# A router's one-hot tiles held behind a weight split, and three row buffers for every later expert, in a fused attention and mixture-of-experts kernel

## The chip, the cores and the metric

One core of a Trainium2 chip runs the whole program in one launch. The metric is the device time of an execution in microseconds; the time of a kernel is the median of several executions on the chip.

## The reference

Three layers follow each other on 8 x 576 = 4608 tokens of 512 channels. The change lies in the second one.

```python
def _attn_ref(q, k, v, phi):          # per batch and head
    a = phi - np.max(phi, axis=2, keepdims=True)
    ...
    k_m = np.einsum('bhsm,bhsd->bhmd', a, k)
    v_m = np.einsum('bhsm,bhsd->bhmd', a, v)
    ...
    return np.matmul(attn, v_m)

def _moe_ref(x, w_gate, w1, w2):      # 8 experts, 576 tokens each
    logits = x @ w_gate
    order = np.argsort(-logits.flatten())
    ...
    for idx in order:                 # best pair first, until an expert is full
        tok, e = (int(idx) // E, int(idx) % E)
        if assigned[tok] >= 0 or counts[e] >= cap:
            continue
        assigned[tok] = e
        counts[e] += 1
    ...
    for e in range(E):
        mask = assigned == e
        h = np.maximum(x[mask] @ w1[e], 0.0)
        out[mask] = h @ w2[e]

def _moe2_ref(x, w_in, w_out):        # dense, 512 to 2048 and back
    h = x @ w_in
    g = h * np.clip(h + 3.0, 0.0, 6.0) / 6.0
    return g @ w_out
```

## The kernel before, in words

The first part (the attention, lines up to 530) writes the rows x to a DRAM tensor xd and keeps the logits LG on the chip. The second part is built by a small planner. The main line issues the matmuls of the experts in order; beside it run generators (routes, gathers, weights, dense_max, dense, and the evictions), which issue their instructions when the planner's clock CK.now says that their inputs are there. So the order in each engine's queue is decided when the program is built, by estimated times; on the chip each engine works through its own queue in that order and waits by semaphores.

Every product is made of float16 pieces: a matrix is scaled by a power of two and split into a high and a low half (the high half by ScalarE, ACT, the low half by VectorE, DVE, as a scalar_tensor_tensor; a few by GpSimd, POOL), and three matmuls take the place of one.

- `route(k)` (L737) finds the expert that fills next and its 576 tokens: eight steps of a search (C, counts on TensorE into rtp, flags FL, mi), then the counts ce, the totals tot, and six one-hot tiles OH of 128 x 768, made by VectorE in `oh` (L926), each followed by six small matmuls OH x RH (L952). From their sum come the row indices ix{k}.
- `gathers` (L1056) fetches the 576 rows of expert k from xd in five indirect transfers issued on POOL (xg), transposes them on TensorE (xp), and splits them into xt. Experts 2 to 7 have two buffers (depth 2): the third transfer waits for the first transpose. Expert 1 has all five at once, three of them in staging buffers of the weights (wst0, wst1), which it borrows.
- `weights` (L984) fetches the weights T = 2k (first layer) and T = 2k+1 (second layer) of expert k in four chunks wst0 to wst3 (POOL transfers), sums their squares, reduces these to one scale s over all partitions (pow2, all_max L688: a matmul amx against the identity), and splits the chunks into w_0 to w_3. The set W2[k] is marked when all four are split. T = 3 waits until expert 1 has its rows under way (XI), since it needs the borrowed buffers.
- `mm_slot` (L631) hands out the four PSUM slots that the layers' tiles, the transposes and the reductions share. MMQ lists who holds one. When four are taken, the next caller takes the oldest entry out of the list and waits for it; while it waits, the generators go on, and one of them can find three entries and take a slot.
- `l1(k)` and `l2(k)` are the two layers of expert k: 16 tiles of 12 matmuls and 8 tiles of 24, so 192 matmuls of 128 x 288 each. Expert 0 takes the first layer four tiles at a time. After two experts, `l34` runs the dense layers on their 1152 tokens; its matmuls need the dense weights, which `dense_piece` (L1206) brings in 32 pieces through VectorE (a shift and three or four cva steps each), in the gaps, with spare buffers named by `spare` (L1147).

Nearly all instructions behind line 550 carry the line of a helper: L567 for VectorE, ScalarE and GpSimd, L618 for the layers' matmuls, L623 for transposes, L694 for the reductions amx.

Of the kernel before, what the change touches and what calls it, by code (L numbers as in the profile page):

```python
# [9 lines left out]
F32 = mybir.dt.float32  # L10
F16 = mybir.dt.float16
BF16 = mybir.dt.bfloat16
# [8 lines left out]
def attn_moe_kernel(ctx: ExitStack, tc: tile.TileContext, q, k, v, phi, w_gate, w1, w2, w_in, w_out, out):  # L21
    nc = tc.nc
# [3 lines left out]
    NT = 36  # L26
# [603 lines left out]

    def mm_slot(done):  # L631
        while len(MMQ) >= 4:
            d = MMQ.pop(0)
            b, CK.busy = CK.busy, False
            need(lambda: d[0])
            CK.busy = b
        MMQ.append(done)

    def mm_tile(shape, name, done):
# [22 lines left out]
    nc.vector.tensor_scalar(triu, jp, 0.0, None, op0=OP.is_lt)  # L662
    onesb = rt.tile([128, 128], BF16, name="onesb")
    nc.vector.memset(onesb, 1.0)
    ones72 = rt.tile([128, 2 * NT], F32, name="ones72")
    nc.vector.memset(ones72, 1.0)
    wE = rt.tile([128, E], F32, name="wE")
    nc.vector.tensor_scalar(wE, iT[:, 0:E], -1.0, float(E), op0=OP.mult, op1=OP.add)
    pb = rt.tile([128, 4], F32, name="pb")
# [67 lines left out]
    def route(k):  # L737
# [121 lines left out]
        else:  # L859
# [11 lines left out]
        V_.scalar_tensor_tensor(G[:, 0], V, thf, be, op0=OP.is_gt, op1=OP.mult)  # L871
        V_.scalar_tensor_tensor(G[:, 1], V, thf, be, op0=OP.is_equal, op1=OP.mult)
        sc = rt.tile([128, 2, NT], F32, name="scn")
        V_.tensor_tensor_scan(sc.rearrange("p a t -> p (a t)"), ones72, G.rearrange("p a t -> p (a t)"), 0.0,
                              op0=OP.mult, op1=OP.add)
        tot = rt.tile([128, 2], BF16, name="tot")
        V_.tensor_copy(tot, sc[:, :, NT - 1])
# [46 lines left out]
        p = ps.tile([128, 64], F32, name="rtp")  # L924

        def oh(q4):  # L926
            o = rt.tile([128, 6, 128], BF16, name="OH", bufs=3)
            V_.tensor_tensor(o, lo[:, 6 * q4:6 * q4 + 6, None].to_broadcast([128, 6, 128]),
                             i128[:, None, :].to_broadcast([128, 6, 128]), op=OP.is_equal)
            return o  # L930
        yield V_.t - 0.3
        OH = [oh(0)]
        if k == 0:
            lof = hbuf(2)[:, 0:6]
# [49 lines left out]
    def weights():  # L984
        for T in range(2 * E):
            k, which = divmod(T, 2)
            while k not in EIX or T == 3 and 1 not in XI:
                yield CK.now + 0.3
            for c in range(4):
                if T == 0 and c == 2:  # L990
# [24 lines left out]
            for n in range(9):  # L1015
                if n < 8:
                    c, i = divmod(n, 2)
                    if i == 0:
                        tl.append(wk.tile([128, 2, 1024], F16, name=f"w{which}_{c}"))
                    cs = slice(i * 512, i * 512 + 512)  # L1020
                    if n in PS.get(T, ()):
                        A_.activation(WST[T, c][0][:, cs], WST[T, c][0][:, cs], AF.Copy, scale=s[:, 0:1])
                        yield A_.t - 0.3
                        A_.activation(tl[c][:, 0, cs], WST[T, c][0][:, cs], AF.Copy)
                    else:
                        A_.activation(tl[c][:, 0, cs], WST[T, c][0][:, cs], AF.Copy, scale=s[:, 0:1])
                    rd.append(A_.t + HOP)
                if n and n - 1 in PS.get(T, ()):
                    yield rd[n - 1], G_
                    c, i = divmod(n - 1, 2)  # L1030
                    cs = slice(i * 512, i * 512 + 512)
                    G_.tensor_tensor(tl[c][:, 1, cs], WST[T, c][0][:, cs], tl[c][:, 0, cs], op=OP.subtract)
                    yield CK.now + 0.1, A_
                    WC[T] = c + i, tl
                elif n:
                    yield rd[n - 1], V_
                    c, i = divmod(n - 1, 2)
                    cs = slice(i * 512, i * 512 + 512)
                    V_.scalar_tensor_tensor(tl[c][:, 1, cs], WST[T, c][0][:, cs], s[:, 0:1], tl[c][:, 0, cs],
                                            op0=OP.mult, op1=OP.subtract)  # L1040
                    if i and T + 1 < 2 * E and T != 2:
                        w_issue(T + 1, c)
                    yield CK.now + 0.1, A_
                    WC[T] = c + i, tl
            yield V_.t
            (W1, W2)[which][k] = tl

    XT, XI = {}, set()

    def ybuf(m):  # L1050
        return wk.tile([128, CAP], F32, name=f"y_{m}")
# [4 lines left out]
    def gathers():  # L1056
        for k in range(E):
# [7 lines left out]
            def fetch(i):  # L1065
                n = 64 if i == 4 and k % 2 == 0 else 128
                if k == 0:
                    xg = hbuf(3 + i)[:, 0:512]
                elif k == 1 and i > 1:
                    if i % 2 == 0:  # L1070
                        big.append(wk.tile([128, 2, 512], F32, name="xg", tag=f"wst{i // 2 - 1}"))
                    xg = big[-1][:, i % 2]
                else:
                    xg = wk.tile([128, 512], F32, name="xg", tag=f"xg{i % 2}")
                G_.indirect_dma_start(out=xg[:n], out_offset=None, in_=xd, in_offset=U(ap=ix[:n, i:i + 1], axis=0))
                rdy.append(dma(0.75, G_.t) + (2.2 if k > 1 else 0.0))
                xgs.append((i, n, xg))
            depth = 2 if k > 1 else 5
            big = []
            if k == 0:  # L1080
                G_.t = max(G_.t, XDT[0])
            for i in range(depth):
# [1 line left out]
                    while not SR[0]:  # L1084
                        yield CK.now + 0.1
                fetch(i)
            XI.add(k)
            while k and L1D.get(k - 1, 0) < 8:
                yield CK.now + 0.3
            xt = wk.tile([128, 2, 4, CAP], F16, name="xt")  # L1090
# [56 lines left out]
    def spare(kind):  # L1147
        tags = ["dst0", "dst1", "dst2"] if kind else ["cva0", "cva1"]
        if 1 in XT or 1 in L1D:
            tags += [] if kind else ["xg0", "xg1"]  # L1150
        if 1 in W2:
            tags += [f"wst{c}" for c in range(4)] if kind else ["wscr"]
        for t in tags:
            if t not in BUSY:
                return t
# [379 lines left out]
```

## Time and profile before

| | us |
|---|---|
| median of 3 runs | 1510.31 (1505.42 to 1511.45) |
| profiled execution | 1503.65 |
| its span | 1501.6 |
| TensorE busy in it | 1397.4 (93%) |
| VectorE busy | 835.3 (56%) |
| ScalarE busy | 732.6 (49%) |
| GpSimd busy | 487.8 (32%) |

The span is what the profiler saw on the core, 2.05 us less than the execution's own time. A busy share is the time in which an engine works on an instruction; waiting in its queue isn't counted. The attention fills about the first 225 us, expert 0 the time to 324 us, expert 1 to 380 us, the dense layers of these two follow, and from some 450 us on the pattern repeats with experts 2 and 3, 4 and 5, 6 and 7.

### The profile page before, as it was taken

The numbers are of one execution on the slowest core, as the hardware profiler recorded it, in microseconds if no ns is written. First come the engines' busy times: TensorE is split into PE (matmuls) and PEld (weight loads), VectorE is DVE, ScalarE is ACT, GpSimd is POOL, SyncE is SP. The second block draws the span as 40 slices with busy tenths as digits, with TensorE's granted clock in tenths as the row PEclk, the third lists the DMA queues.
The fourth block names the chain that finished last, engine by engine and source line by source line (L and its number), as shares of the span: only waits on it lengthen the run. The fifth ranks groups of instructions, "written<-read, shape, count | busy, mean of one in ns | idle before, by whom it ended". The sixth has DMA issues, their size and how long they took to land.

```text
span 1501.6 us, 26275 instructions
## 1 busy us (share of the span) xinstructions
PE 1397.4 (93%) x10506; PEld 931.4 (62%) x10506; DVE 835.3 (56%) x1985; ACT 732.6 (49%) x1419; POOL 487.8 (32%) x555
## 2 busy tenths in 40 slices
PE   4778886898889999999999999999999999999997
PEld 3667764777444555997555558875555588755553
DVE  4788967889995775553146755522459335221111
ACT  3667655577763563452335634523346445233332
POOL 3565305134553443301233532102325421023232
PEclk9989996999999999999999999999999999999999
DMA  9866587355310221200001311100013211000000
GB/s 299 293 231 201 158 273 248 118 185 167 114 43 22 82 84 57 86 28 2 1 22 57 109 57 51 64 1 1 22 57 110 71 39 62 1 0 22 1 21 21
DMA packets 65913, 130.67 MB, mean 87 GB/s; under 512 B 5248, under 2 KB 35968, under 8 KB 65792
## 3 DMA queue, kind: packets, MB, share of 16 engines
q1 hardware_dynamic: 49808, 74.48, 15.0%
q0 software_dynamic: 15168, 52.96, 10.9%
q8 instruction: 82, 1.34, 0.4%
q10 hardware_dynamic: 816, 1.57, 0.3%
q14 instruction: 39, 0.32, 0.1%
HBM read 110.12 MB, written 18.87 MB: 86 GB/s over the span
## 4 chain that ended last, share of the span: by engine, by line
PE 67%; DVE 14%; ACT 5%; issue 5%; DMA 4%; POOL 2%; SPq 0%; ACTq 0%; POOLq 0%; DVEq 0%
PE p L618 39%; PE acc L618 21%; DVE cva L567 4%; DMA xg<-xd,ix 2%; PE xa L420 1%; DMA ph<-in_phi_dram 1%; PE kvp L191 1%; DMA wst<-in_moe_w_dram,ei 1%; DVE w L567 1%; ACT h L567 1%; PE rtp L795 1%; DVE pm L138 1%; PE xp L623 1%; DVE h L567 1%; POOL h L567 1%
## 5 line engine op out<-in xcount | busy, mean ns | idle before, releaser
L618 PE MATMUL acc<-wo,h 128*128 128x512 f16 x1728 | 418.1, 379 | 5.2 <-ACT h L567 4.3
L618 PE MATMUL p<-yt,wi 128*128 128x384 f16 x2304 | 417.6, 327 | 0.0
L567 POOL TENSOR_TENSOR h<-h,h 128x384 f16<-128x384 f32 x192 | 187.3, 976 | 634.5 <-ACT h L567 492.6
L618 PEld LDWEIGHTS <-w 128*128 128x128 f16 x3072 | 339.1, 121 | 49.1 <-issue 4.4
L618 PEld LDWEIGHTS <-wi 128*128 128x128 f16 x2304 | 219.2, 98 | 156.0 <-issue 1.2
L567 ACT ACTIVATE h<-p,half_c,inv 128x384 f32<-128x384 f32 (+1 forms) x256 | 143.9, 587 | 278.5 <-PE p L618 271.2
L618 PEld LDWEIGHTS <-h 128*128 128x128 f16 x1728 | 163.5, 98 | 174.1 <-ACT h L567 6.0
L567 DVE SCALAR_TENSOR_TENSOR h<-h,p 128x384 f32<-128x384 f32 x192 | 105.9, 551 | 290.0 <-ACT h L567 282.7
L618 PE MATMUL p<-xt,w 128*128 128x288 f16 x1536 | 198.8, 289 | 3.7 <-DVE h L567 3.5
L618 PE MATMUL p<-h,w 128*128 128x288 f16 x1536 | 196.3, 287 | 4.3 <-DVE w L567 3.7
L567 ACT ACTIVATE h<-h 128x384 f16<-128x384 f32 x192 | 100.1, 521 | 135.7 <-DVE h L567 131.9
L567 DVE SCALAR_TENSOR_TENSOR h<-p,h 128x288 f16<-128x288 f32 x128 | 57.4, 455 | 73.6 <-ACT h L567 73.5
L567 DVE SCALAR_TENSOR_TENSOR w<-wst,s,w 128x512 f16<-128x512 f32 x124 | 96.1, 806 | 2.2 <-ACT w L567 2.2
L567 POOL DMA_INDIRECT wst<-in_moe_w_dram,ei x64 | 68.7, 1073 | 87.0 <-DVE scn L567 33.5
L567 ACT ACTIVATE h<-p 128x288 f16<-128x288 f32 x128 | 51.7, 410 | 90.8 <-PE p L618 90.8
L567 ACT ACTIVATE w<-wst,s 128x512 f16<-128x512 f32 x124 | 82.5, 712 | 7.1 <-DVE s L567 6.2
L567 DVE SCALAR_TENSOR_TENSOR cva<-dst,cva 128x512 int32<-128x512 int32 (+1 forms) x96 | 82.7, 881 | 0.5 <-ACT dst L567 0.3
L567 DVE TENSOR_REDUCE ym<-y 128x1 f32<-128x288 f32 x64 | 28.8, 450 | 91.5 <-ACT y L567 91.3
L567 ACT ACTIVATE wscr<-wst 128x1024 bf16<-128x1024 f32 x64 | 67.3, 1052 | 13.3 <-DMA wst<-in_moe_w_dram,ei 12.6
L567 ACT ACTIVATE y<-p 128x288 f32<-128x288 f32 x64 | 26.1, 407 | 96.6 <-PE p L618 95.1
L567 POOL DMA_INDIRECT xg<-xd,ix x35 | 37.2, 1064 | 75.9 <-PE xp L623 49.7
L191 PE MATMUL kvp<-kvt,A 128*64 128x128 f32 x576 | 46.0, 315 | 7.3 <-ACT A L170 3.3
(313 smaller groups left out, 1558.4 us busy)
## 6 DMA issues: line engine op xcount, KB each, us to landing
dst<-in_moe_w_out_dram SPq DMA_DIRECT2D x26, 512.0 KB, 4.3
qt<-in_q_dram SPq DMA_DIRECT2D x8, 1024.0 KB, 11.5
dq<-in_moe_w_in_dram SPq DMA_DIRECT2D x16, 512.0 KB, 5.7
xd<-xs SPq DMA_DIRECT2D x32, 256.0 KB, 5.5
kvt<-in_k_dram SPq DMA_DIRECT2D x7, 1152.0 KB, 9.1
kvt<-in_v_dram SPq DMA_DIRECT2D x7, 1152.0 KB, 11.8
dst<-in_moe_w_in_dram SPq DMA_DIRECT2D x15, 512.0 KB, 4.0
ph<-in_phi_dram SPq DMA_DIRECT2D x8, 576.0 KB, 9.8
```

Source lines behind the costliest of these rows:

```text
L138: nc.vector.tensor_reduce(pm, PH[b].rearrange("p h (r m) -> p h m r", m=M), axis=AX.X, op=OP.max)
L191: nc.tensor.matmul(p[i * 64:(i + 1) * 64, g, 0:128], A[:, hp, r, :], KV[b][:, :, hp, r * 64:(r + 1) * 64], start=(r == 0), stop=(r == R - 1))
L420: nc.tensor.matmul(p[r, g], AT[u][:, half, g, r], VB[b][:, g], start=True, stop=True)
L567: r = f(*a, **kw)
L618: nc.tensor.matmul(o, l, r, start=start, stop=stop)
L623: nc.tensor.transpose(o, i, idn)
L795: nc.tensor.matmul(p[:60, :32], C[:, 4 * t:4 * t + 4].rearrange("p t n -> p (t n)"), Bo[:, 4 * t:4 * t + 4].rearrange("p t e -> p (t e)"), ...
```

## The change

Four edits go together. In `mm_slot` a waiting caller leaves the oldest entry in the list until it is done. In `route`, the second round (k = 1) makes its one-hot tiles only after W2[0], the split second weights of expert 0, is marked, and OH has two buffers instead of three. In `gathers` every expert from 1 on has three buffers xg0 to xg2; nothing is borrowed, so `weights` drops the wait for XI and asks for T = 3 as each chunk of T = 2 is split. The third row buffer also becomes a spare buffer for cva. A tile of 72 ones gives way to columns of ones_c.

```diff
     def mm_slot(done):
         while len(MMQ) >= 4:
-            d = MMQ.pop(0)
+            d = MMQ[0]
             b, CK.busy = CK.busy, False
             need(lambda: d[0])
             CK.busy = b
+            if MMQ and MMQ[0] is d:
+                MMQ.pop(0)
         MMQ.append(done)
...
-    ones72 = rt.tile([128, 2 * NT], F32, name="ones72")
-    nc.vector.memset(ones72, 1.0)
...
         def oh(q4):
-            o = rt.tile([128, 6, 128], BF16, name="OH", bufs=3)
+            o = rt.tile([128, 6, 128], BF16, name="OH", bufs=2)
...
         yield V_.t - 0.3
+        while k == 1 and 0 not in W2:
+            yield CK.now + 0.1
         OH = [oh(0)]
...
-            while k not in EIX or T == 3 and 1 not in XI:
+            while k not in EIX:
                 yield CK.now + 0.3
...
-                    if i and T + 1 < 2 * E and T != 2:
+                    if i and T + 1 < 2 * E:
                         w_issue(T + 1, c)
...
-                elif k == 1 and i > 1:
-                    if i % 2 == 0:
-                        big.append(wk.tile([128, 2, 512], F32, name="xg", tag=f"wst{i // 2 - 1}"))
-                    xg = big[-1][:, i % 2]
                 else:
-                    xg = wk.tile([128, 512], F32, name="xg", tag=f"xg{i % 2}")
+                    xg = wk.tile([128, 512], F32, name="xg", tag=f"xg{i % 3}")
...
-            depth = 2 if k > 1 else 5
-            big = []
+            depth = 3 if k else 5
...
-            tags += [] if kind else ["xg0", "xg1"]
+            tags += [] if kind else ["xg0", "xg1", "xg2"]
```

The orders that the planner makes of it differ from the first layer of expert 0 on. On TensorE, before, the reduction for the scale of expert 0's second weights (amx from s_0m) stands between two groups of four layer tiles:

```order
L618 MATMUL p_3822<-xt,w_3_3652 128x288
L618 LDWEIGHTS w_3_3652
L618 MATMUL p_3822<-xt,w_3_3652 128x288
L694 MATMUL amx<-ident,s_0m 128x128
L813 LDWEIGHTS onesb
L813 MATMUL rtp<-FL,onesb 128x8
L618 LDWEIGHTS w_0_3574
L618 MATMUL p_3945<-xt,w_0_3574 128x288
```

Now it stands 46 layer matmuls further on, inside the next group, between the last tile's matmuls:

```order
L618 MATMUL p_3948<-xt,w_3_3650 128x288
L618 LDWEIGHTS w_3_3650
L618 MATMUL p_3959<-xt,w_3_3650 128x288
L694 MATMUL amx<-ident,s_0m 128x128
L618 LDWEIGHTS w_3_3650
L618 MATMUL p_3959<-xt,w_3_3650 128x288
L618 LDWEIGHTS w_3_3650
L618 MATMUL p_3959<-xt,w_3_3650 128x288
L795 LDWEIGHTS C
```

What moved is amx, from behind 96 to behind 142 of the 192 matmuls of that layer.

On VectorE, before, the end of the second routing round (RH, then the one-hot tiles OH) runs on with only steps of the dense pieces (cva) and maxima of y between the tiles; the halves w_0 to w_3 of expert 0's second weights stand some thirty rows ahead of this:

```order
L567 TENSOR_SCALAR lo<-sli 128x36
L567 TENSOR_SCALAR hi<-sli 128x36
L567 TENSOR_TENSOR R_4274<-hi,iTf 128x180
L567 TENSOR_TENSOR RH<-R_4274,idt 128x360
L567 TENSOR_TENSOR OH<-lo,i_2717 128x768
L567 SCALAR_TENSOR_TENSOR cva<-dst,cva 128x512
L567 TENSOR_REDUCE ym<-y_4171 128x1
L567 TENSOR_TENSOR OH<-lo,i_2717 128x768
L567 SCALAR_TENSOR_TENSOR cva<-dst,cva 128x512
L567 TENSOR_TENSOR OH<-lo,i_2717 128x768
```

Now the last two pairs of these halves, w_2 and w_3, stand between RH and the first one-hot tile:

```order
L567 TENSOR_SCALAR lo<-sli 128x36
L567 TENSOR_SCALAR hi<-sli 128x36
L567 TENSOR_TENSOR R_4213<-hi,iTf 128x180
L567 TENSOR_TENSOR RH<-R_4213,idt 128x360
L567 SCALAR_TENSOR_TENSOR w_2_4151<-wst_3673,s_0_3901,w_2_4151 128x512 x2
L567 SCALAR_TENSOR_TENSOR w_3_4219<-wst_3697,s_0_3901,w_3_4219 128x512 x2
L567 SCALAR_TENSOR_TENSOR cva<-dst,cva 128x512
L567 TENSOR_TENSOR OH<-lo,i_2717 128x768
L567 TENSOR_SCALAR cva<-dst 128x512
L567 TENSOR_TENSOR OH<-lo,i_2717 128x768
```

The one-hot tiles, and with them the six groups of matmuls on TensorE, follow the split; on TensorE the first group stands behind 15 matmuls of the second layer of expert 0, where it stood behind 63.

On POOL, before, the five gathers of expert 1's rows stand together, and the four transfers of its second weights behind them:

```order
L567 DMA wst_4236<-in_moe_w_dram,ei_4187 128x1024
L567 TENSOR_TENSOR wi_4267<-cva,wi_4267 128x512
L567 TENSOR_TENSOR wi_4402<-cva,wi_4402 128x512
L567 DMA xg<-xd,ix_4466 128x512 x5
L567 DMA wst_4592<-in_moe_w_dram,ei_4187 128x1024
L567 DMA wst_4603<-in_moe_w_dram,ei_4187 128x1024
```

Now three gathers stand together, then a subtraction of a dense piece (wi), then the other two and the first two weight transfers:

```order
L567 DMA wst_4243<-in_moe_w_dram,ei_4170 128x1024
L567 TENSOR_TENSOR wi_4266<-cva,wi_4266 128x512
L567 DMA xg<-xd,ix_4411 128x512 x3
L567 TENSOR_TENSOR wi_4404<-cva,wi_4404 128x512
L567 DMA xg<-xd,ix_4411 128x512 x2
L567 DMA wst_4509<-in_moe_w_dram,ei_4170 128x1024
L567 DMA wst_4542<-in_moe_w_dram,ei_4170 128x1024
L567 TENSOR_TENSOR wo_4526<-cva,wo_4526 128x512
```

The fourth and fifth gather moved behind that subtraction, and subtractions of dense pieces now stand among the weight transfers.

## Rows read from the trace of the kernel before

**Rows 1.** Windows: stretch, length; busy PE, PEld, DVE, ACT, POOL; PE clock, DMA, GB/s.

```profile
274.00:299.20 25.20, 21.55 (x182) 18.23 (x183) 21.71 (x67) 11.10 (x22) 4.95 (x5) 1.00 0.25 77
299.20:312.70 13.50, 13.08 (x132) 9.96 (x130) 13.05 (x31) 9.53 (x19) 3.04 (x2) 1.00 0.58 205
312.70:324.60 11.90, 9.35 (x76) 7.40 (x74) 9.58 (x20) 7.10 (x14) 6.77 (x7) 1.00 0.47 125
324.60:357.60 33.00, 27.71 (x219) 25.83 (x217) 31.80 (x64) 27.95 (x59) 12.18 (x10) 1.00 0.49 160
357.60:389.60 32.00, 26.93 (x196) 19.86 (x196) 31.86 (x52) 22.33 (x40) 15.61 (x11) 0.95 0.61 195
389.60:446.40 56.80, 51.89 (x268) 26.29 (x269) 55.97 (x79) 40.35 (x71) 32.61 (x26) 0.97 0.22 65
450.00:1501.60 1051.60, 1037.79 (x6977) 654.81 (x6975) 463.72 (x1147) 445.61 (x858) 293.14 (x313) 1.00 0.13 41
```

**Rows 2.** Waits of TensorE, 225 to 450 us: total us, times, longest.

```profile
PE amx L694 <- DVE sy_1m L567: 5.5, 1, 5.5
PE acc L618 <- ACT h L567: 4.3, 4, 1.8
...
PE p L618 <- DVE w L567: 3.7, 2, 2.3
```

**Rows 3.** Waits of TensorE, 450 us to the end.

```profile
PE xp L623 <- DMA xg<-xd,ix: 2.1, 4, 1.0
PE rtp L855 <- DVE ce L567: 1.7, 1, 1.7
```

**Rows 4.** Timeline of TensorE, 225 to 330 us: start, us, instruction, wait.

```profile
274.48 0.49 PE L694 MATMUL amx<-ident,s_0m 128*128 128x128 f32 x2 [1.11 <-DVE h L567]
...
277.62 2.00 PE L618 MATMUL p<-xt,w 128*128 128x288 f16 x15 [1.00 <-DVE h L567]
...
285.11 1.14 PE L618 MATMUL p<-xt,w 128*128 128x288 f16 x8 [1.43 <-DVE h L567]
...
292.88 0.28 PE L618 MATMUL p<-h,w 128*128 128x288 f16 x1 [0.61 <-ACT h L567]
...
296.26 4.57 PE L618 MATMUL p<-h,w 128*128 128x288 f16 x36
...
310.22 0.31 PE L952 MATMUL rtp<-RH,OH 128*128 128x10 bf16 x6 [0.24 <-DVE dmm L567]
...
316.23 0.63 PE L623 MATMUL xp<-ident,xg 128*128 128x128 f32 x4 [0.92 <-DMA xg<-xd,ix]
...
324.37 2.12 PE L618 MATMUL p<-xt,w 128*128 128x288 f16 x16
```

**Rows 5.** Timeline of VectorE, 232 to 330 us.

```profile
277.49 1.41 DVE L567 SCALAR_TENSOR_TENSOR w<-wst,s,w 128x512 f16<-128x512 f32 x2
...
299.24 0.95 DVE L567 TENSOR_TENSOR OH<-lo,i 128x768 bf16<-128x768 int32 x1
```

**Rows 6.** Timeline of GpSimd (POOL): first gather of expert 1.

```profile
312.84 0.97 POOL L567 DMA_INDIRECT xg<-xd,ix  x1 [3.49 <-DVE ix L567]
```

**Rows 7.** Windows of the cva steps on VectorE alone: busy us (steps), clock, DMA.

```profile
357.60:389.60 32.00, 28.70 (x37) 0.95 0.61 195
389.60:446.40 56.80, 45.39 (x53) 0.97 0.22 65
```

**Rows 8.** Timeline of TensorE, 326 to 452 us.

```profile
441.11 2.12 PE L618 MATMUL acc<-wo,h 128*128 128x512 f16 x9 [1.84 <-ACT h L567]
...
445.39 1.47 PE L618 MATMUL acc<-wo,h 128*128 128x512 f16 x6 [0.22 <-ACT h L567]
447.19 0.82 PE L618 MATMUL acc<-wo,h 128*128 128x512 f16 x3 [0.33 <-POOL h L567]
```

**Rows 9.** Windows around the wait at sy_1, columns as in Rows 1.

```profile
384.60:390.00 5.40, 0.04 (x1) 0.00 (x0) 5.26 (x16) 4.50 (x9) 2.38 (x2) 0.96 0.42 145
390.00:391.50 1.50, 1.41 (x5) 0.98 (x6) 1.50 (x4) 0.52 (x1) 0.46 (x1) 0.50 0.05 11
```

More of the change, by code (lines that the diff above doesn't have):

```diff
@@ L873, in route @@
         sc = rt.tile([128, 2, NT], F32, name="scn")
-        V_.tensor_tensor_scan(sc.rearrange("p a t -> p (a t)"), ones72, G.rearrange("p a t -> p (a t)"), 0.0,
+        V_.tensor_tensor_scan(sc.rearrange("p a t -> p (a t)"), ones_c[:, 0:2 * NT], G.rearrange("p a t -> p (a t)"), 0.0,
                               op0=OP.mult, op1=OP.add)
@@ L1046, in weights @@
             (W1, W2)[which][k] = tl
-    XT, XI = {}, set()
+    XT = {}
     def ybuf(m):
@@ L1086, in gathers @@
                 fetch(i)
-            XI.add(k)
             while k and L1D.get(k - 1, 0) < 8:
```

## The prediction

> **What bounds the kernel now.** I read the stretches first. From 450 us to the end TensorE (PE) is busy 1037.79 of 1051.60 us, at full clock. From 274 to 446.4 us it is VectorE (DVE) that hardly rests: it idles 3.49, 0.45, 2.32, 1.20, 0.14 and 0.83 us in the six stretches [rows 1]. So a change in the early stretch is paid in VectorE's queue, and one in the late stretch only where TensorE still waits. The waits agree: between 225 and 450 us TensorE lost 5.5 us ahead of the reduction for sy_1 (the scale of the second expert's output), 3.7 us for weight halves and 4.3 us for h tiles of the dense layers [rows 2]; after 450 us the row buffers cost it 2.1 us in four waits, the counts ce 1.7 us [rows 3]. What the edited lines can win is part of some 20 us of idle time before 450 us and of some 4 us after it.
>
> On TensorE the two programs are alike until 274 us. From there I replay the new order with the durations of the trace; positions are counted in the orders of the engines.
>
> **1. The slot rule: the second scale of expert 0 comes later.** Before, the reduction matmul for s_0 of the second weights (amx) stood behind 96 of the 192 first-layer matmuls and started at 274.48, after a wait of 1.11 us for a slot; the layer then waited 1.00 and 1.43 us for its own slots [rows 4]. Now a waiting tile of the layer keeps its place in the list, the reduction can't get in front of it, and amx stands behind 142 matmuls. The layer goes on at 273.9 instead of 275.0; its fourth tile waits for a slot until 276.3 (1.15 us, 9 matmuls done). 37 matmuls of 0.127 us (36 in 4.57 us [rows 4]), the small routing matmuls between them (0.8 us) and a wait of 0.85 us for amx's own slot put it at about 282.7, 8.2 us later. The dense reduction (dmm), which now stands two layer matmuls behind it, takes a second slot, and the next tile waits 1.1 us. In all the slots cost 3.4 us, as much as the 3.5 us before.
>
> **2. The split of those weights meets the router on VectorE.** Eight halves (two in 1.41 us [rows 5]) stood between 277.5 and 289. Now one pair stands behind the last routing step, one behind ce and two behind RH, and the gate puts the first one-hot tile (OH) behind them all. VectorE's load up to there is nearly the same (0.75 us more in small reductions, some 0.5 us less idle). The first OH, 0.95 us from 299.24 before [rows 5], ends at about 300.6: 0.4 us later.
>
> **3. TensorE stands still ahead of it.** The first layer of expert 0 ends at 291.9, the router's totals cost 0.95 us, and the second layer begins at 293.1 (before 292.88 [rows 4]). It runs 14 matmuls and waits for w_2, which follows RH: until 297.3, 2.35 us. One matmul later stands the first OH group, behind 15 second-layer matmuls where it stood behind 63: it waits until 300.7, 3.3 us. The other five groups come at TensorE's own pace (62 matmuls, 0.31 us a group [rows 4]). The last stands at 310.1, as before (310.22), but with 77 second-layer matmuls done instead of 125: 48 x 0.127 = 6.1 us behind.
>
> **4. Rows of expert 1.** The first gather can go out at 311.4 instead of 312.84 [rows 6], since fewer other steps stand between the last OH group and the indices. From that issue to the transpose at 316.23 it took 3.4 us [rows 4, 6]. With three buffers the first three go out at 311.4, 312.7 and 314.0; the last two need a buffer back, stand behind a POOL subtraction, and go out at 316.4 and 317.7. The transposes at 315.4, 316.6, 318.0, 319.9 and 321.2 cost about 2 us of waits, as many as before. The second expert's first layer, 324.37 before [rows 4], starts at 330.1: **5.7 us late**.
>
> **5. What VectorE makes of that.** Ahead of sy_1 now stand eight more steps of the dense pieces (cva), which fall into the gap that TensorE leaves. At 0.78 us a step (37 in 28.70 us), less the overlap of neighbours, 0.66; in the late stretch 0.86 (53 in 45.39 us [rows 7]): 5.3 to 6.9 us. Against them VectorE had 7.6 us of idle time up to 389.6, the first five figures of [rows 1]; in the replay 6.5 us of it remain (3 before the first OH, 2 at the transposes, 1.5 in the first layer of expert 1). So sy_1 is 5.3 - 1.1 = **4.2 us late**, at worst 5.8. TensorE's 5.7 us are not added: it waited 3.7 us for halves and 5.5 us at sy_1 [rows 2], and a late start fills these waits. If nothing of VectorE's idle time remained, sy_1 would be 2.3 us early: the lower bound.
>
> **6. The tail.** The eight steps are gone from the end, where h tiles queue behind them: TensorE's waits of 1.84, 0.22 and 0.33 us from 441 us on [rows 8] fall. The other h waits, 4.3 - 1.84 - 0.22 = 2.2 us, stand in an unchanged order and stay. **2.4 us back.**
>
> **7. Experts 2 to 7.** Three gathers stand in front where two stood; the fourth and fifth follow together. That can take at most the 2.1 us of row waits [rows 3]; the fourth still waits for a buffer. I take **1.3 us back**, between 0 and 3.8 (with ce, which moves too).
>
> At nothing: the removed memset of 72 columns (ahead of the router, nobody waits); two OH buffers (the third tile needs the first group's matmuls, over 2 us before it); the earlier request for expert 1's second weights (needed after 350); a third spare buffer for cva (pieces wait for VectorE, not for room). If the room were what held them, that is the faster rival.
>
> **Sum:** 4.2 - 2.4 - 1.3 = +0.5 us. The profiled execution took 1503.65 us, so 1504.2 on its scale; it lies 6.7 us under the median of the runs, 1510.31, and the runs spread over 6.0 us. The prediction is for a median: **1510.8 us**. I take 0.5%, 7.5 us, as what a measurement of this kernel can tell from no change.
>
> **A row against the change.** TensorE did 0.04 us of work from 384.6 to 390, and from 390 to 391.5 the granted clock was 0.50, the level of 1.2 GHz [rows 9]; by 393 this had cost 1.5 us. The new wait ahead of OH, 2.35 and 3.3 us with one matmul between, is alike. My sum leaves it out, since the matmuls behind it are tied to OH tiles; at half clock 11 of them take 2.8 us against some 1.9 us a tile, so up to 1.5 us could show. The Trainium skill (TensorE: Matmul & The Clock Gate, Part 1: The HAM clock gate) says that the throttled state is the default and that activity lifts it, so a long wait is paid twice. By that rule the sum is 0.5 + 1.5 = +2.0 us; the row at 390 agrees with it.
>
> **Rivals.**
> - *Slower: the late start is not filled.* It decides at VectorE's first h step of expert 1's first layer, near 332 us. If VectorE has run dry there, everything behind it, the second weights of expert 1 and sy_1, moves by the whole 5.7 us, and the clock is lost twice, behind OH and behind a longer wait at sy_1 (1.5 us each); the tail's gain is eaten by the pieces that then run late. +8.7 us, 1519. For it: the h steps stand in order and nothing overtakes them. Against: the replay finds VectorE busy with pieces until 331.6. Chance 0.22.
> - *Faster: VectorE's idle time goes.* A third spare buffer lets a third piece be in flight; if that fills all but 3 of the 7.6 us, sy_1 is 5.3 - 4.6 = 0.7 us late, all 4.3 us of h waits go, 3.8 us after 450, and the 1.5 us of low clock behind sy_1: -8.9 us, 1501.4. Against: much of the idle time is a wait for routing matmuls, and these stay. Chance 0.24.
> - *The gate does nothing*, the weights being split before the router gets there. VectorE's order speaks against it: w_2 and w_3 stand between RH and OH. Steps 3 and 5 would vanish: -1.3 us, within 0.5%. Chance 0.04.
>
> **The numbers.** The forecast has 0.50. The rivals lie just beyond 0.5%: of the faster one 0.20 falls outside, of the slower one 0.17, and of the forecast, by the spread of the runs, 0.05 on either side. So faster 0.25, slower 0.22, the rest 0.53. The range takes in the centres of both rivals and a little more, 1500 to 1520; beyond it I leave about 0.2.
>
> **What would show it.** Right: amx for s_0 at 281 to 284; TensorE waiting over 5 us between 294 and 301, for w and then OH; the first layer of expert 1 at 329 to 332; a wait at sy_1 that ends 2 to 6 us later; no h wait behind 441; under 1.5 us of row waits after 450. Wrong in size: a clock near 0.5 at 300 to 305, or VectorE idle by over 2 us near 332. Wrong in kind: OH groups spread over the second layer as before, or TensorE's position at 450 more than 6 us off.

## The result and the profile after

| | us |
|---|---|
| median of 7 runs, changed kernel | 1516.68 (1515.76 to 1521.18) |
| median of 7 runs, kernel before, same chip | 1506.16 (1501.62 to 1511.45) |
| ratio | 1.0068, 95% interval 1.0046 to 1.0089 |
| profiled execution and its span | 1515.76 and 1513.9 |

The changed kernel is slower by 0.68%, some 10 us. Against the runs of before beside it that is +10.5 us where +0.5 was forecast (1510.8 us, on a median of three runs that lay 4 us over the seven here). The time lies inside the range that was given, 1500 to 1520, only because that range took in the centre of the slower rival, at +8.7; the forecast's own sum missed by 10 us, so the hit of the range is luck as far as its mechanism goes.

The profiled executions don't start the experts at the same time: the first product of l1(0), up to which TensorE's order has not changed, stands at 253.78 us before and at 256.03 now. Such differences come with every profile here (the eleven below have it between 251.50 and 256.51; whether the change has a part in it isn't shown). So I count from that product, and call its time t; "on the old scale" means 2.25 us taken off. From t to the end of the span it is 1501.6 - 253.78 = 1247.8 us before and 1513.9 - 256.03 = 1257.9 now, 10.1 us more: the whole loss.

The windows of the changed kernel (columns as in [rows 1]) for the stretches behind the split of expert 0's second weights:

```profile
274.00:292.00 18.00, 15.77 (x135) 13.38 (x134) 16.21 (x50) 8.97 (x18) 1.52 (x1) 1.00 0.30 90
292.00:300.00 8.00, 3.81 (x29) 2.74 (x27) 7.62 (x27) 2.73 (x6) 0.00 (x0) 0.98 0.00 0
300.00:309.00 9.00, 6.78 (x54) 4.87 (x55) 8.22 (x13) 2.32 (x4) 7.96 (x4) 0.64 0.47 127
309.00:316.00 7.00, 3.66 (x40) 2.74 (x37) 0.00 (x0) 1.27 (x3) 1.94 (x2) 1.00 0.78 290
316.00:323.00 7.00, 5.08 (x27) 3.30 (x28) 5.55 (x16) 5.75 (x12) 1.80 (x2) 0.55 0.00 0
...
450.00:1513.90 1063.90, 1051.64 (x7054) 661.88 (x7052) 470.31 (x1157) 452.23 (x871) 295.23 (x320) 1.00 0.12 41
```

The new row is the fourth: in 309 to 316 VectorE, which idled 0.45 us in the whole of its second stretch of [rows 1], does nothing at all for 7 us. TensorE works at 0.64 and 0.55 of its clock on either side of it. The late stretch is as full as before.

The timeline of TensorE before, three rows that [rows 4] doesn't have: the first product of l1(0), the start of l2(1), and the reduction for sy_1.

```profile
253.78 0.46 PE L618 MATMUL p<-xt,w 128*128 128x288 f16 x1
...
350.86 2.25 PE L618 MATMUL p<-h,w 128*128 128x288 f16 x17
...
390.09 0.77 PE L694 MATMUL amx<-ident,sy_1m 128*128 128x128 f32 x2 [5.45 <-DVE sy_1m L567]
```

The timeline of TensorE now, with these rows and those that answer to [rows 4]:

```profile
256.03 0.46 PE L618 MATMUL p<-xt,w 128*128 128x288 f16 x1
...
285.20 0.49 PE L694 MATMUL amx<-ident,s_0m 128*128 128x128 f32 x2 [0.87 <-DVE h L567]
...
294.55 1.88 PE L618 MATMUL p<-h,w 128*128 128x288 f16 x14 [0.18 <-DVE h L567]
...
298.76 0.30 PE L618 MATMUL p<-h,w 128*128 128x288 f16 x1 [2.33 <-DVE w L567]
...
302.22 0.32 PE L954 MATMUL rtp<-RH,OH 128*128 128x10 bf16 x6 [3.16 <-DVE OH L567]
...
310.63 0.30 PE L954 MATMUL rtp<-RH,OH 128*128 128x10 bf16 x6
...
317.92 0.32 PE L954 MATMUL rtp<-RH,OH 128*128 128x10 bf16 x6 [5.26 <-DVE OH L567]
...
340.57 4.08 PE L618 MATMUL p<-xt,w 128*128 128x288 f16 x32
...
366.90 2.24 PE L618 MATMUL p<-h,w 128*128 128x288 f16 x17
...
406.27 0.76 PE L694 MATMUL amx<-ident,sy_1m 128*128 128x128 f32 x2 [5.04 <-DVE sy_1m L567]
```

The waits of 2.33 and 3.16 us for w_2 and for the first one-hot tile are there as forecast. The fifth group comes at 310.63, and then the sixth is 5.26 us late. From there on everything is late, and by the same amount: l1(1) starts at t + 84.5 where it started at t + 70.6, l2(1) at t + 110.9 where it started at t + 97.1, and the reduction for sy_1 stands at t + 150.2 where it stood at t + 136.3.

What held the sixth tile can be followed over three queues. GpSimd (POOL) first, the four loads of expert 1's first weights in the kernel before, with the first and the last load of its second weights behind them:

```profile
294.19 0.95 POOL L567 DMA_INDIRECT wst<-in_moe_w_dram,ei  x1 [7.69 <-DVE ei L567]
295.45 0.94 POOL L567 DMA_INDIRECT wst<-in_moe_w_dram,ei  x1 [0.30 <-issue]
296.69 0.94 POOL L567 DMA_INDIRECT wst<-in_moe_w_dram,ei  x1 [0.30 <-issue]
297.94 0.94 POOL L567 DMA_INDIRECT wst<-in_moe_w_dram,ei  x1 [0.30 <-issue]
...
322.14 0.94 POOL L567 DMA_INDIRECT wst<-in_moe_w_dram,ei  x1 [2.54 <-DMA xg<-xd,ix]
...
327.18 0.95 POOL L567 DMA_INDIRECT wst<-in_moe_w_dram,ei  x1 [0.30 <-issue]
```

and in the changed kernel the same loads:

```profile
300.13 5.54 POOL L567 DMA_INDIRECT wst<-in_moe_w_dram,ei  x1 [18.04 <-DVE w L567]
305.97 1.10 POOL L567 DMA_INDIRECT wst<-in_moe_w_dram,ei  x1 [0.30 <-DVE ym L567]
307.37 1.16 POOL L567 DMA_INDIRECT wst<-in_moe_w_dram,ei  x1 [0.30 <-issue]
308.84 0.94 POOL L567 DMA_INDIRECT wst<-in_moe_w_dram,ei  x1 [0.30 <-issue]
...
329.65 0.94 POOL L567 DMA_INDIRECT wst<-in_moe_w_dram,ei  x1 [0.30 <-issue]
...
339.48 0.94 POOL L567 DMA_INDIRECT wst<-in_moe_w_dram,ei  x1 [0.30 <-issue]
```

Before, they waited for the row table (ei) alone, since the buffers wst0 to wst3 had long been given back by the split of the second weights of expert 0. Now they wait for that split (18.04 us, `<-DVE w`). And they stand in a bad order, as the order of GpSimd's queue and of ScalarE's shows (wst_4230 is chunk 0, wst_4243 chunk 1, wst_4222 chunk 2, wst_4227 chunk 3). It comes from `weights`: each split asks for the next load into its own buffer, but the splits of w_0 and w_1 came before the row table, so nothing was asked for there; the splits of w_2 and w_3 then asked for chunks 2 and 3, and chunks 0 and 1 came last.

```
POOL  DMA wst_4222, DMA wst_4227, DMA wst_4230, DMA wst_4243
ACT   wscr<-wst_4230, y<-p, wscr<-wst_4243, wscr<-wst_4222, wscr<-wst_4227, y<-p
```

Chunks 0 and 1 were free when VectorE had split w_1 at 292.6, and the row table was there at 293.2. But their loads are queued behind that of chunk 2, which waits for w_2. ScalarE takes the square sums (wscr) of chunk 0 first, and a y copy stands behind them. ScalarE and VectorE in the changed kernel:

```profile
314.73 1.06 ACT L567 ACTIVATE wscr<-wst 128x1024 bf16<-128x1024 f32 x1 [9.01 <-DMA wst<-in_moe_w_dram,ei]
315.70 0.19 ACT L567 ACTIVATION_READ_ACCUMULATOR wscr<-wst 128x1 f32 x1
315.79 0.39 ACT L567 ACTIVATE y<-p 128x288 f32<-128x288 f32 x1
```

```profile
307.64 0.95 DVE L567 TENSOR_TENSOR OH<-lo,i 128x768 bf16<-128x768 int32 x1
316.21 0.45 DVE L567 TENSOR_REDUCE ym<-y 128x1 f32<-128x288 f32 x1 [7.62 <-ACT y L567]
316.58 0.42 DVE L567 TENSOR_SCALAR cva<-dst 128x512 int32<-128x512 int32 x1
316.91 0.95 DVE L567 TENSOR_TENSOR OH<-lo,i 128x768 bf16<-128x768 int32 x1
```

So a load for which ScalarE waits 9.01 us holds a square, the square a y copy, the copy a maximum on VectorE for 7.62 us, and the maximum the sixth one-hot tile. Whether this stall is the loss, or only its visible sign, the rows can't tell: the late loads also push expert 1's first weights, and with them the loads of its second weights, which use the same four buffers (the last of them issued at t + 83.5 instead of t + 73.4).

### The profile page after: what moved, and what is told of

The parts are those of the page before. It is cut to its first block, busy times and chain, and to the rows that moved or that the text cites. A ratio compares the mean times of both kernels' runs of the same rounds, so it can differ in the third digit from the quotient of the medians.

```text
span 1513.9 us, 26278 instructions
## 1 busy us (share of the span) xinstructions
PE 1403.9 (93%) x10506; PEld 933.9 (62%) x10506; DVE 833.9 (55%) x1984; ACT 731.1 (48%) x1419; POOL 488.4 (32%) x556
## 4 chain that ended last, share of the span: by engine, by line
PE 71%; DVE 14%; ACT 4%; DMA 4%; issue 4%; POOL 2%; SPq 0%; ACTq 0%; POOLq 0%; DVEq 0%
PE p L618 41%; PE acc L618 21%; DVE cva L567 5%; PE xa L420 2%; DMA xg<-xd,ix 1%; DMA ph<-in_phi_dram 1%; PE kvp L191 1%; PE rtp L795 1%; POOL h L567 1%; PE xp L623 1%; DVE h L567 1%; DVE w L567 1%; ACT h L567 1%; DVE pm L138 1%; DMA wst<-in_moe_w_dram,ei 1%
## 5 line engine op out<-in xcount | busy, mean ns | idle before, releaser
L618 PE MATMUL p<-h,w 128*128 128x288 f16 x1536 | 201.1, 292 | 6.8 <-DVE w L567 6.6
L567 ACT ACTIVATE h<-h 128x384 f16<-128x384 f32 x192 | 100.1, 521 | 135.6 <-DVE h L567 128.1
L567 DVE TENSOR_REDUCE ym<-y 128x1 f32<-128x288 f32 x64 | 28.8, 450 | 97.1 <-ACT y L567 97.1
```

The source lines that it names most:

```text
L567: r = f(*a, **kw)
L618: nc.tensor.matmul(o, l, r, start=start, stop=stop)
```

## The experiments

Four theories. **A**: the slot rule makes the loss, because the late scale of expert 0's second weights lets the loads through the buffers wst0 to wst3 fall behind. **G**: the gate does, by putting OH tiles behind the split. **R**: the three row buffers do. **C**: ScalarE's order does, a square ahead of a y copy. Each run is compared with runs of the kernel before on the same chip; a ratio is over these, with its 95% interval.

### The old slot rule in the changed kernel

```diff
     def mm_slot(done):
         while len(MMQ) >= 4:
-            d = MMQ[0]
+            d = MMQ.pop(0)
...
-            if MMQ and MMQ[0] is d:
-                MMQ.pop(0)
```

> The changed kernel with the slot rule of before (the waiting entry leaves the list first); the gate, the two OH buffers and the three row buffers stay. Theory A (the slot rule makes the loss: the scale of expert 0's second weights is late, the weights are split by the router, and with them the loads of expert 1's first weights, whose first one now starts at 300.1 and lands at 314.7 where before it started at 294.2 and landed at 298.8): the first of these loads starts at 294 to 295, the first product of l1(1) stands at 324 to 327, the time is within 0.3 % of before (1502 to 1511). Rival R (the three row buffers and what they do to VectorE's order make it): the time stays over 1512 with l1(1) as early as before.

Measured: 1506.03 us, ratio 0.9997 (0.9975 to 1.0019). The loss is gone; the first load starts at 297.95 with t = 256.51, so at t + 41.4 (before t + 40.4). With the old rule the gate has nothing to wait for, so this is the kernel with the row buffers, the earlier requests and the two OH buffers alone: R falls. One part was not as expected: l1(1) starts at 333.32, t + 76.8, since a maximum for sy_0 now stands ahead of the last two row tiles of expert 1. TensorE's timeline of this run:

```profile
331.05 0.77 PE L692 MATMUL amx<-ident,sy_0m 128*128 128x128 f32 x2 [4.58 <-DVE sy_0m L567]
331.61 1.91 PE L623 MATMUL xp<-ident,xg 128*128 128x128 f32 x8
333.32 4.88 PE L618 MATMUL p<-xt,w 128*128 128x288 f16 x25
```

So l1(1) is 6.2 us late here, and the time doesn't show it: a first hint that the start of l1(1) isn't what sets the end. It is no more than a hint, since the row buffers can win something that hides it (below they do).

### The changed kernel without the gate

```diff
-        while k == 1 and 0 not in W2:
-            yield CK.now + 0.1
```

> The changed kernel without the two lines that make route 1's OH tiles wait for expert 0's second weights; the new slot rule stays. Theory A: nothing is won, since the scale is as late as in the changed kernel; the last two pieces of the weights now take turns with OH tiles on VectorE, so that the loads of expert 1's first weights start 1 to 4 us later than 300.1; 1515 to 1522. Rival G (the gate makes the loss: OH tiles behind the weights let TensorE stand 3.2 us and its clock fall): OH tiles come at 298, the stall is gone, 1505 to 1511.

Measured: 1514.25 us, ratio 1.0045 (1.0026 to 1.0064). Slower than before as well, just under the 1515 to 1522 that A expected, and not told apart from the changed kernel (the intervals overlap). The first OH group stands at 298.95, 3.3 us earlier, and nothing is won. The loads start at t + 45.8 to t + 53.1, as late as in the changed kernel (t + 44.1 to 52.8). G falls.

### Squares later, loads unchanged

```diff
                 st, ready = WST[T, c]
-                yield ready, A_
+                yield ready + (9.0 if T == 2 and c == 0 else 0.0), A_
```

> The changed kernel with the four squares of expert 1's first weights planned 9 us later, so that they stand behind l2(0)'s next y copies on ScalarE; loads as in the changed kernel. Theory A in its form 'the load is late' (the chain load, squares, scale, weights sets the start of l1(1)): the sixth OH tile comes without the 5.3 us wait, but l1(1) still starts at 337 to 343, since its loads land at 314.7 and its weights follow some 20 to 26 us behind; 1513 to 1518. Rival C (ScalarE's order makes it: a square that waits 9.0 us for its load holds the y copy, this the VectorE, this the sixth OH tile): 5 us and most of the second half-clock stretch come back, 1506 to 1511.

Measured: 1517.31 us, ratio 1.0067 (1.0046 to 1.0088). The sixth OH group no longer waits 5.26 us (0.65), and l1(1) starts at t + 79.6, 4.9 us earlier than in the changed kernel (I had expected 337 to 343 on its scale, t + 81 to t + 87). Nothing of it reaches the end, which speaks against C. It doesn't rule C out, since the planner also moved two of the squares behind row tiles, so that the second weights' last load came later still, at t + 85.8: what one edit gave back, the other may have taken. The runs with late second loads below lose without that wait.

### Loads in the order of their buffers

```diff
                     if i and T + 1 < 2 * E:
-                        w_issue(T + 1, c)
+                        for cc in range(c + 1):
+                            w_issue(T + 1, cc)
```

> The changed kernel with the loads of the next weights issued in the order of their buffers (the first two, whose buffers are free at 292.5, no longer queue on GpSimd behind the two that wait for VectorE at 300.1). Theory A: the first load starts at 293 to 295 and lands near 299, the last starts near 302 and lands near 308 (6.5 us before 314.7), the sixth OH tile loses most of its 5.3 us wait, l1(1) starts at 331 to 336 instead of 340.6; 1507 to 1512. Rival G (the gate makes the loss) and rival R (row buffers): no change from the changed kernel, 1514 to 1519.

Measured: 1505.82 us, ratio 0.9994 (0.9976 to 1.0012). A loop of one line, and the loss is gone within the interval, with the new slot rule, the gate and the late scale left as they are; l1(1) starts at 334.62, as expected, and the time is a little under what I had expected. The last load was to start near 302; it starts at 306.01, behind one whose row takes 5.52 us. GpSimd's timeline of this run:

```profile
294.00 0.96 POOL L567 DMA_INDIRECT wst<-in_moe_w_dram,ei  x1 [11.87 <-DVE scn L567]
295.26 0.94 POOL L567 DMA_INDIRECT wst<-in_moe_w_dram,ei  x1 [0.30 <-ACT w L567]
300.19 5.52 POOL L567 DMA_INDIRECT wst<-in_moe_w_dram,ei  x1 [3.98 <-issue]
306.01 1.11 POOL L567 DMA_INDIRECT wst<-in_moe_w_dram,ei  x1 [0.30 <-DVE ym L567]
```

The loads of chunks 0 and 1 are out at t + 38.4 and t + 39.7, where the changed kernel had them at t + 51.3 and t + 52.8; the other two come 0.5 us later than their counterparts there. The sixth OH group stands at 312.69 without a wait, and the last load of the second weights at t + 75.6. TensorE's wait of 3.16 us for the first OH tile is still there, and so is the low clock behind it, as the windows of this run show:

```profile
294.00:300.00 6.00, 2.36 (x17) 1.48 (x16) 5.75 (x18) 1.16 (x2) 1.90 (x2) 1.00 0.55 175
300.00:306.00 6.00, 3.72 (x27) 2.48 (x28) 5.63 (x10) 2.53 (x4) 5.52 (x1) 0.50 0.31 91
```

So a stall and six microseconds at the 1.2 GHz level cost nothing that this run shows. The interval reaches from 3.6 us faster to 1.8 us slower, and the row buffers may win something in it, so a price of a microsecond or two isn't excluded.

### The kernel before, with late loads of the second weights

These runs were made to separate two forms of A. In the slower kernels both l1(1) and the second weights' loads are late; here only the loads are.

```diff
         for T in range(2 * E):
...
+            if T == 3:
+                while L1D.get(1, 0) < 2:
+                    yield CK.now + 0.1
+                e2 = rt.tile([128, 4], I32, name="ei2")
+                V_.tensor_copy(e2, EIX[1])
+                EIX[1] = e2
             for c in range(4):
```

> The kernel before, with one thing made late: the four loads of expert 1's second weights read a copy of the row table that VectorE makes only when two of eight blocks of l1(1) have been planned. Slot rule, gate, buffers and the loads of the first weights as before. Theory A, now in the form that the four runs suggest (all weights go through four load buffers, one set after the other, and what the end hangs on is the last load of expert 1's second weights: it starts 73.4 us behind the first product of l1(0) before, 71.6 and 75.6 in the two runs that cost nothing, 81.8, 83.5 and 85.8 in the three that cost 7 to 10): the last load starts 79 to 83 us behind, l1(1) starts as before (70 to 72), sy_1's maximum comes 6 to 12 us later than 136.3, the time is 5 to 10 us over before. Rival L (the late start of l1(1) is the loss, 70.6 before, 79 to 85 in the slow runs): within 2 us of before.

Measured: 1512.82 us, ratio 1.0043 (1.0027 to 1.0060). With 3 in place of 2:

> As the run with the second loads late, but behind three blocks of l1(1): the loads start some 3 us later again. Theory A: 2 to 4 us slower than that run, so 8 to 13 us over before. Rival L: within 2 us of before.

Measured: 1515.99 us, ratio 1.0060 (1.0041 to 1.0079). Nothing of the change is in these two kernels but lateness of one set of loads, and what the planner makes of it; they lose 0.43% and 0.60% of 1505.3, 6.5 and 9.0 us. GpSimd's timeline of the second one (t = 251.50), first and last load, and the start of l1(1) and the reduction for sy_1 on its TensorE:

```profile
332.60 0.96 POOL L567 DMA_INDIRECT wst<-in_moe_w_dram,ei  x1 [2.30 <-DVE cva L567]
...
337.03 0.94 POOL L567 DMA_INDIRECT wst<-in_moe_w_dram,ei  x1 [0.31 <-issue]
```

```profile
320.68 2.12 PE L618 MATMUL p<-xt,w 128*128 128x288 f16 x16
...
402.28 0.76 PE L694 MATMUL amx<-ident,sy_1m 128*128 128x128 f32 x2 [5.09 <-DVE sy_1m L567]
```

l1(1) starts at t + 69.2, even earlier than before. The last load is at t + 85.5, 12.1 us later than before, and sy_1 at t + 150.8, 14.5 us later. So a loss of this size needs no late start of l1(1) (rival L of the expectation): late loads of the second weights are enough for it. What they change is also VectorE's order. The planner fills the time with dense pieces: 93 cva steps, 70.3 us, run between t and the reduction for sy_1, where before 76 ran, 55.5 us, and VectorE idles hardly more than before (12.7 us against 10.4). Whether it is the wait for the weights or these steps in front of the maxima that makes sy_1 late, the two runs don't separate.

### A version that wins

The first run had the change's row buffers without its slot rule, and lost time only to a maximum for sy_0 in a bad place. Planned 4 us later:

```diff
-        sy = yield from pow2(a, f"sy_{k}", False, 15, 2, 3.0 * (k % 2 and k > 1))
+        sy = yield from pow2(a, f"sy_{k}", False, 15, 2, 4.0 if k == 0 else 3.0 * (k % 2 and k > 1))
```

> The changed kernel with the slot rule of before, and the maximum for sy_0 planned 4 us later: it stood in front of the last two row tiles of expert 1, where TensorE waited 4.6 us for it (first run). Theory A: l1(1) starts 3 to 5 us earlier than in that run (72 to 74 behind l1(0)'s first product instead of 76.8); since the second weights' last load is not late there (71.6), the end gains at most what sy_1's maximum was later than before (140.2 against 136.3): 1502 to 1506. Rival: VectorE bounds this stretch and nothing is gained, 1505 to 1508.

Measured: 1499.56 us, ratio 0.9957 (0.9939 to 0.9975), 5.7 us faster than the 1505.3 of before and better than I had expected. GpSimd's timeline of this run (t = 252.65), the second weights' loads:

```profile
316.06 1.02 POOL L567 DMA_INDIRECT wst<-in_moe_w_dram,ei  x1 [0.31 <-issue]
317.38 0.94 POOL L567 DMA_INDIRECT wst<-in_moe_w_dram,ei  x1 [0.30 <-issue]
321.45 0.94 POOL L567 DMA_INDIRECT wst<-in_moe_w_dram,ei  x1 [0.30 <-issue]
322.70 1.11 POOL L567 DMA_INDIRECT wst<-in_moe_w_dram,ei  x1 [0.31 <-DVE ymx L567]
```

They no longer wait for expert 1's rows to give borrowed buffers back, and the last one is out at t + 70.0, 3.4 us earlier than before. To see whether the one line does it alone, it was put into the kernel before, with nothing of the change:

> The kernel before with the one line of the run that planned sy_0's maximum later, and nothing of the change: five row buffers with two borrowed, its slot rule. It says whether the 0.43 % that run won come from the line alone. If the gain is the change's own other half (row buffers of its own, loads of the second weights no longer held back by borrowed buffers, which start their last load at 70.0 instead of 73.4 behind l1(0)'s first product): within 2 us of before, as there is no wait for sy_0 in its TensorE rows. If the line itself wins: 1498 to 1502.

Measured: 1511.12 us, ratio 1.0028 (1.0011 to 1.0045). The line alone wins nothing; it loses 0.28%, more than the 2 us that I had allowed, and why was not followed up (TensorE waits 6.1 us for halves there, 3.7 before [rows 2]). So the gain needs both: the row buffers alone win nothing (the first run, 0.9997), the line alone loses, and together they win 0.43%.

### Loads in order, without the gate

> The changed kernel with the loads in the order of their buffers, and without the gate. Theory A: the first two loads start near 294 as in the run with the gate, the last two at 302 and 304 behind the pieces that take turns with OH tiles; the second weights' last load starts 73 to 78 us behind l1(0)'s first product; 1504 to 1509, no difference that the gate makes. Rival G (the gate, by letting TensorE stand for OH tiles, costs what is left): 3 us or more faster than the run with the gate (under 1503).

Its edits are those of the run without the gate and of the run with ordered loads. Measured: 1513.62 us, ratio 1.0055 (1.0037 to 1.0073). Neither expectation was right. With the loads in order the gate is not idle but worth having: without it the last halves w_2 and w_3 take turns with OH tiles on VectorE, l2(0) starts at t + 47.8 instead of t + 39.0, and the second weights' last load comes at t + 78.9 instead of t + 75.6. So G has the wrong sign as well, and loads in order are not enough by themselves.

### All eleven profiles side by side

All in us behind t; the end is the span less t. Worked out from the timelines of each run as above, sorted by the third column.

| kernel | t | last load of second weights | l1(1) starts | sy_1 | end |
|---|---|---|---|---|---|
| row buffers, sy_0 later | 252.65 | 70.0 | 73.5 | 135.6 | 1243.2 |
| row buffers, old slot rule | 256.51 | 71.6 | 76.8 | 140.2 | 1248.7 |
| before, sy_0 later | 252.94 | 72.7 | 69.9 | 137.5 | 1250.7 |
| **before** | 253.78 | 73.4 | 70.6 | 136.3 | 1247.8 |
| change, loads in order | 255.58 | 75.6 | 79.0 | 138.1 | 1248.5 |
| the same without the gate | 256.24 | 78.9 | 80.8 | 146.8 | 1253.8 |
| change without the gate | 256.09 | 81.8 | 80.0 | 150.5 | 1257.7 |
| before, second loads late | 252.72 | 82.6 | 70.3 | 145.4 | 1254.9 |
| **change** | 256.03 | 83.5 | 84.5 | 150.2 | 1257.9 |
| before, second loads later | 251.50 | 85.5 | 69.2 | 150.8 | 1259.3 |
| change, squares later | 252.23 | 85.8 | 79.6 | 152.1 | 1260.2 |

The end goes with the last load in the large: 1243.2 to 1250.7 where it is out by 75.6, 1253.8 to 1260.2 where it comes later. The medians fall into the same two groups, ratios of 0.9957 to 1.0028 and of 1.0043 to 1.0068; "before, sy_0 later" stands out, whose median is 0.28% over before with its last load on time. It doesn't go with the start of l1(1), which is 69.2 in one of the slowest and 79.0 in a kernel that lost nothing. From the last load to the reduction for sy_1 it takes 62.5 to 68.7 us in all eleven, and from there to the end 1107.0 to 1113.2.

That the last load goes with the end doesn't make it the carrier in every kernel. In the chain of work that ended last, followed back by the profile, a load of the second weights stands in the kernel before (issued at 324.31, 5.22 us) and in the two kernels with late second loads (331.09, 5.67 us, and 335.11, 7.84 us), and also with ordered loads but no gate (335.18, 8.93 us). In the changed kernel none does: its chain runs over the load of the first weights issued at 307.37 (7.34 us), the square, the y copy, two gathers (4.66 and 4.17 us), a load of a dense piece (7.28 us) and VectorE's own queue. So shown are the cause, loads through wst0 to wst3 that come late (taking the lateness away by order or by the old slot rule takes the loss away, and making loads late makes a loss), and that late second loads suffice. By which of the two sets of loads the delay of the changed kernel reaches sy_1 is not shown; both are late there.

## Why the prediction was right and wrong

- **Step 1, right.** amx for s_0 stands at t + 29.17 (285.20); the forecast of 282.7 was t + 28.9. The waits for slots were smaller than worked out, 0.20, 0.99 and 0.87 us, 2.1 in all against 3.4.
- **Step 2, right as far as it went.** The first OH tile ends at 302.16, that is 299.9 on the scale of the trace before; 300.6 was forecast. What the step left out is below.
- **Step 3, half right.** The waits ahead of the first OH group, 2.33 and 3.16 us, were forecast as 2.35 and 3.3. Then "the other five groups come at TensorE's own pace" failed at the sixth: it stands at 317.92, 315.7 on the old scale, not 310.1. I had followed VectorE's and TensorE's queues, but not ScalarE's, where the squares of expert 1's first weights stand ahead of a y copy.
- **Step 4, mis-sized by that.** l1(1) was to start at 330.1 and started at 340.57, 338.3 on the old scale: 13.9 us late instead of 5.7.
- **Step 5, the step that failed.** sy_1 was to be 4.2 us late, 5.8 at worst; it is 13.9. The eight more cva steps are there (84 between t and sy_1, before 76), and they cost 4.6 us of VectorE's time against 5.3 in the sum. What failed is the other term, VectorE's idle time, which was to fall by 1.1 us: it rose by 8.8, from 10.4 to 19.2 us between t and sy_1, and 7.62 of that is one wait, at the end of the three queues behind the late load. The sum had no wait for a load in it, and it held the loads of the second weights at nothing ("the earlier request for expert 1's second weights (needed after 350)"). The request isn't earlier: its last load moved from t + 73.4 to t + 83.5. That TensorE's late start would fill its own waits failed too: it waits 1.36 and 2.89 us for halves in l2(1) and 5.04 us at sy_1, as before.
- **The omission behind it.** Step 2 moves the end of the split from 289 to 300, and prices what TensorE waits for. It doesn't ask what the split gives back: the four load buffers, nor in which order the loads into them are asked for. Their next loads started at t + 44.1 instead of t + 40.4, the second of them at t + 49.9 instead of t + 41.7, and both sets of expert 1's weights came late. With the loads in order the loss is gone (1505.82 us).
- **Steps 6 and 7, right in the sum, not in its terms.** From sy_1 to the end the changed kernel takes 1107.6 us, before 1111.5: 3.9 us back, and 3.7 were forecast. But the tail gave back 0.6 us, not 2.4: from sy_1 to the first routing matmul of the next pair, 318 matmuls on, it is 66.0 us against 66.6, since the h waits behind 441 us did not vanish (1.64 us and 1.29 us remain, at 448.28 and 457.54). The other 3.3 us came behind 508 us, where 1.3 were forecast: the counts ce are no longer among the waits and the rows cost 1.2 us instead of 2.1. These are one profile of each kernel; without the change's row buffers that stretch took 1108.5 to 1113.2 us in four profiles, with them 1107.0 to 1110.4 in seven.
- **The clock.** The price of 1.5 us for a low clock behind the OH wait, which the Trainium skill (TensorE: Matmul & The Clock Gate, Part 1: The HAM clock gate) spoke for, was left out of the sum. The clock did fall, to 0.50 between 300 and 306 us, longer than I had allowed. The run with ordered loads has the same row and no loss beyond its interval, so a cost of it isn't shown here; the rule tells the clock, not what it costs.
- **The slower rival** was near in time (1519 forecast, 1516.68 measured) and right in its consequence, that l1(1), sy_1 and what lies between move by the whole delay. That its time came near is luck: its delay was 5.7 us, not 13.9, and the rest of its sum, 3 us for the clock, no run shows (the sum also leaves out the 1.3 us of step 7). It was wrong in its place and cause: VectorE ran dry at 308.6 for 7.62 us, not near 332, and behind a load, not behind TensorE's late start. That a late start of l1(1) costs 5.7 us by itself no run shows: two kernels with the row buffers had it 6.2 and 8.4 us late and lost nothing.
- **The faster rival** named VectorE's idle time and a third spare buffer. There is a gain with the three row buffers, but VectorE idles nearly as long in it (9.3 us against 10.4); what its rows show instead is loads of the second weights that don't wait for borrowed buffers, 3.4 us earlier. No run makes these loads early alone.
- **Its own signs.** "Wrong in kind" was to be TensorE over 6 us off at 450: that first routing matmul stands 13.3 us late (472.31 and 456.72, less 2.25). The rival that the gate does nothing fell: the halves w_2 and w_3 start at 297.96 on VectorE, ahead of the first OH tile at 301.21.

## What to carry to other kernels

When a step that empties a buffer is moved, price the next load into that buffer, and follow it to whoever waits for its data, before pricing the engines around the step; here a wait of 3.2 us and six microseconds at half clock cost nothing that could be measured, and late loads cost 10 us. In an in-order queue, put transfers in the order in which their buffers come free and their readers take them: one that must wait holds all behind it. A late part of an early stage is found by sorting all runs by one candidate time after the other; the one that sorts the ends as well is the one to make late by itself in the kernel before, and the chain of each trace then tells whether it is the carrier there.

## What was not expected of the hardware

The issue of one indirect load on GpSimd, 0.94 to 0.95 us in the rows of before, took 5.54 us in the changed kernel (300.13), 5.52 with ordered loads (300.19) and 5.54 with later squares. It is not only a rough span, since the next load starts only at 305.97. But it isn't the time until that load moves either: in the changed kernel DMA carries nothing from 300 to 302 us, 200 GB/s from 302 to 304 and 75 from 304 to 306, some 550 KB, about the 512 KB of that load, and before as well little moves in the first two microseconds behind a first issue (12 GB/s from 294 to 296). VectorE is busy without a gap from 300 until 304.84, and in all three kernels the row ends within 0.1 us of the end of the maximum of y (ym) behind that gap. The Trainium skill (SBUF — State Buffer, SBUF: two separate sides) says that VectorE, in some of its modes, can keep GpSimd from writing the descriptors of a transfer, for the length of that one instruction. The longest VectorE instruction there is 0.95 us, and before, four loads went out in 0.94 us each beside a VectorE that was busy 1.90 to 1.93 of every 2.00 us. So the rule, for one instruction, doesn't give these 5.5 us; whether several in a row could isn't shown, and no run here was made to find their cause. It is about half of the delay of the second load: the first starts 3.7 us later than before, the second 8.3.
